# The planner of a fused RWKV7 + GELU kernel gets other constants, other load order and other places for its padding

## The chip, the cores and the metric

The kernel runs on one core of a Trainium2 chip. All times are device microseconds of that core, from the runs and from one profiled execution. The kernel before took 725.19 us (median of three runs, 724.26 to 728.75).

The engines are named as the profile names them: PE is TensorE (PEld its weight loads), DVE is VectorE, ACT is ScalarE, POOL is GpSimd, SP is SyncE, which here does nothing but issue DMAs. "Issue" in the profile is time in which an engine waited for nothing that the profile shows.

## The reference

An RWKV7 recurrence over 768 time steps for 4 x 8 heads of size 40, then an MLP of 320 -> 2048 -> 320 with quick GELU over its 3072 tokens. All in float32; the MLP's weights arrive as float64.

```python
for t in range(S):
    kt, vt, rt = (k[:, :, t], v[:, :, t], r[:, :, t])
    wt, at, bt = (w[:, :, t], a[:, :, t], b[:, :, t])
    y[:, :, t] = np.einsum('bhd,bhde->bhe', rt, state)
    Sa = np.einsum('bhde,bhe->bhd', state, at)
    state_decay = state * wt[:, :, None, :] - np.einsum('bhd,bhe->bhde', Sa, bt)
    state = state_decay + np.einsum('bhd,bhe->bhde', vt, kt)
...
h = x @ w_in
g = h * (1.0 / (1.0 + np.exp(-1.702 * h)))
return (g @ w_out).astype(np.float32)
```

## The kernel before

**Tiling.** The recurrence is cut into 12 chunks of 64 steps; each chunk has two units (a unit is half of the batch), so there are 24 units. Unit i needs the state that unit i-2 left. For each unit the kernel forms cumulative decays (`ps_cum`, `ps_cumc`), scores (`ps_A`, `ps_N`, `ps_RV`), the inverse of a triangular matrix in five levels (`ps_level`, then `ps_Q`, `ps_T`), the read of the old state (`ps_zT`, `ps_rz`), the right-hand side (`ps_B`), its solution (`ps_X`) and the output (`ps_y`). The output goes to DRAM (`x_dram`, line 917) and comes back transposed (`xT_all`, line 921). When both units of a chunk are back, the MLP of the chunk can run: 160 x 2 matmuls `ps_up`, the GELU on ACT (`g`), and twice 64 x 2 matmuls `ps_down`.

**Weights.** The MLP's weights come in eight pieces of 1.31 MB each, as float64 (lines 398 to 448). Each piece is loaded into a spare place, turned by ACT (line 422), and then by DVE in five steps (lines 426, 430, 431, 434 and 438). Line 438 is the last one: the piece is usable after it. Pieces 0 to 3 are for `ps_up`, pieces 4 to 7 for `ps_down`. All of this happens in the first 130 us.

**Loads.** A unit's inputs are `ak`, `time`, `b`, `rv` and `RV`, issued by SP in the function `load`; `logw` and `wc` are issued in `load_w`. `ak`, `b` and `rv` fill only 40 of each 64 rows; the other rows stay zero, so the two buffers of each are zeroed once at the start (`padded`, line 306). Before, the three first buffers are zeroed on DVE and the three second ones on POOL, as the last thing of POOL's constants. SP issues in order: a DMA that has to wait for a buffer holds all that follow it.

**The order of the work.** The kernel is fully unrolled, and the order of the instructions on every engine is worked out when it is built. The class `Plan` holds a list of tasks with durations and dependences and plays them through on a picture of the chip: `order` starts, at each moment, the task of best rank that is ready. `paced` repeats this four times with other release times for the MLP's tasks and keeps the pass whose picture ends first. Then the instructions are issued in the order of that pass. So the constants of the picture do not run on the chip; they only decide what comes after what. On the chip each engine runs its list in order, and stops where an operand is not there yet.

The picture has four parts that matter here. `FETCH` is the time in which TensorE's instruction stream gets its next block of `BLOCK` = 256 instructions, and `BESIDE` lengthens it by a share of the time that data transfers run beside it. `LATENCY`, `RATE` and `SPREAD` give the time from the issue of a DMA to its landing. `BEGIN` says from when each engine is free. A task has a `release` before which it may not start; for loads it is zero before.

```python
BLOCK, FETCH, BESIDE, AHEAD = 256, 3550.0, 0.4, 300.0
...
BEGIN = {"PE": 0.0, "ACT": 3300.0, "DVE": 4100.0, "POOL": 9500.0, "SP": 800.0}
LATENCY, RATE, SPREAD = 1200.0, 400.0, 1.3
```

Of the kernel before, what the change touches and what calls it, by code (L numbers as in the profile page):

```python
# [23 lines left out]
ACT = mybir.ActivationFunctionType  # L24
# [34 lines left out]
class Plan:  # L59
# [2 lines left out]

    BLOCK, FETCH, BESIDE, AHEAD = 256, 3550.0, 0.4, 300.0
    DELAY = {"PE": 300.0, "DVE": 60.0, "ACT": 60.0, "POOL": 150.0, "SP": 800.0}

    BEGIN = {"PE": 0.0, "ACT": 3300.0, "DVE": 4100.0, "POOL": 9500.0, "SP": 800.0}
    LATENCY, RATE, SPREAD = 1200.0, 400.0, 1.3

    def __init__(self, slots, pairs):
        self.slots, self.pairs = slots, pairs
        self.tasks, self.made, self.used, self.of_pair = [], {}, {}, {}

    def add(self, rank, engines, fn, reads=(), uses=(), writes=(), room=(), pair=None, most=None, size=0):

        t = Task(rank, engines, fn, pair, most, size)
        for key in uses:  # L80
            self.used.setdefault(key, []).append(t)
        for key in reads:
            t.after.update(self.made[key])
            self.used.setdefault(key, []).append(t)
        for name, n in (*writes, *room):
            if name in self.slots:
                old = (name, n - self.slots[name])
                t.after.update(self.made.get(old, ()), self.used.get(old, ()))
        for key in writes:
            self.made.setdefault(key, []).append(t)  # L90
        if pair is not None:
            writers = self.of_pair.setdefault(pair, [])
            t.after.update(o for o in writers if "PE" in o.engines)
            writers.append(t)
        t.after.discard(t)
        self.tasks.append(t)

    def order(self):
# [11 lines left out]
        running, last = [], {}  # L110

        def fits(t):
            if t.pair is None or t.pair in held:
# [7 lines left out]
        issued, begun, shared = 0, 0.0, 0.0  # L121

        def fetch(at):
            took = self.FETCH
            for _ in range(3):
                beside = sum(max(0.0, min(y, at + took) - max(x, at)) for x, y in running[-8:])
                took = self.FETCH + self.BESIDE / self.SPREAD * beside
            return took

        def unread(t, e):  # L130

            return max((x + 60.0 for o, x in last.get(t.pair, {}).items() if o != e), default=0.0) if t.pair is not None and e != "PE" else 0.0

        def fetched(t, start):

            at, left, ns, block = start, t.instr, t.engines["PE"] / t.instr, begun
            room = self.BLOCK - issued % self.BLOCK
            while left >= room:
                at += room * ns
                left -= room  # L140
                at = block = max(at, block + fetch(block))
                room = self.BLOCK
            return at + left * ns, block

        def ahead(t):

            return (issued % self.BLOCK + t.instr) * fetch(begun) / self.BLOCK - (now + t.engines["PE"] - begun)

        while coming or able:
            while coming and coming[0][0] <= now:  # L150
# [2 lines left out]
            took = None  # L153
# [12 lines left out]
            t = took  # L166
# [2 lines left out]
            end = now + t.engines[e]  # L169
            if e == "PE":  # L170
                end, begun = fetched(t, now)
                issued += t.instr
            if e == "POOL" or e == "DVE" and t.sbuf:

# [2 lines left out]
            free[e] = end  # L177
            if e == "SP":
                wire = max(wire, end + self.LATENCY)
                running.append((wire, wire + self.SPREAD * t.size / self.RATE))  # L180
                end = wire = running[-1][1]
            if t.pair is not None:
                if e != "PE":
# [42 lines left out]
def rwkv7_gelu_quick(ctx: ExitStack, tc: tile.TileContext, time_d, v_d, w_d, wc_d, ak_d, b_d, rv_d, w_in, w_out, out):  # L226
    nc = tc.nc
# [31 lines left out]
    def single(name, shape):  # L259
        return const.tile(shape, FP32, tag=name, name=name)  # L260
# [44 lines left out]
    def padded(engine, t):  # L305
        engine.memset(t, 0.0)
# [10 lines left out]
    nc.vector.tensor_add(two32, one32, one32)  # L317
    padded(nc.vector, b_t[0])
    padded(nc.vector, rv_t[0])

    def select(t, compare, base, sign, fill):

# [13 lines left out]
    for t in logw_t:  # L336
        nc.gpsimd.memset(t[:, DM:], 0.0)

    starts = single("starts", [128, 8, 33])
    nc.gpsimd.memset(starts, 1.0)  # L340
    nc.gpsimd.memset(starts[:, :, 0], 0.0)

    quads, within = single("quads", [128, 2, 32]), single("within", [128, 2, 32])
    nc.gpsimd.memset(quads, 0.0)
# [9 lines left out]
        for p in HALF:  # L354
            select(t[p, :64], ALU.is_gt, 0, 1, 0.0)

    for t in ak_t[1], b_t[1], rv_t[1]:
        padded(nc.gpsimd, t)

    def mask(t):  # L360
        return t.unsqueeze(1).unsqueeze(1).to_broadcast([128, 2, 4, 64])
# [100 lines left out]
    def load_w(i):  # L462
        for name, of, src, n in (("wc", wc_of, wc_d, 528), ("logw", logw_of, w_d, DM))[i < BY_PE:]:
            plan.add(-2 if i == 2 else 10 * i - 30, {"SP": 350.0}, lambda t, of=of, src=src: nc.sync.dma_start(of(i), src[i]),
                     writes=[(name, i)], size=128 * n * 4)

    def load(i):
        for name, of, src, n in (("ak", ak_of, ak_d, 1024), ("time", time_of, time_d, 2 * DM), ("b", b_of, b_d, 512),
                                 ("rv", rv_of, rv_d, 1024), ("RV", RV_of, v_d, 320)):
            rows = [slice(p.start, p.start + D) for p in HALF] if name in ("ak", "b", "rv") else [slice(0, 128)]  # L470

            def go(t, name=name, of=of, src=src, rows=rows):
                for p in rows:
                    dst = of(i)[p, 8:].rearrange("p g j n -> p (g j n)") if name == "RV" else of(i)[p]
                    nc.sync.dma_start(dst, src[i, p])
# [612 lines left out]
```

## Time and profile before

| | us |
|---|---|
| median of 3 runs | 725.19 |
| the profiled execution, device time | 728.5 |
| its span, first to last instruction | 726.7 |
| PE busy in the span | 677.6 |
| DVE busy | 430.0 |
| ACT busy | 356.8 |
| POOL busy | 187.9 |
| mean granted TensorE clock | 0.978 |

The profile page gives for the whole span the busy time of each engine, then slices, DMA queues, the chain of work that ended last, and groups of instructions by line. A table of stretches gives the same busy times for chosen parts of the span; the numbers in brackets are counts of instructions, PEclk is the granted TensorE clock as a share of full speed, then come the mean busy share of the 16 DMA engines and the GB/s that they moved. The chain of waits lists start, duration and what ran, one piece after another.

A busy PE is not PE at its peak, since matmuls overlap and their ends are modelled. Where a number of "PE work" is given, it is the number of matmuls times the time from start to start that the same form has in long runs at full clock: `ps_up` x160 take 8.63 us (54 ns each), `ps_down` x224 15.07 us (67 ns), `ps_y` x64 1.43 us (22 ns), and the forms of 64 columns and less x32 0.46 us (14.5 ns).

### The profile page before, as it was taken

The numbers are of one execution on the slowest core, as the hardware profiler recorded it, in microseconds if no ns is written. First come the engines' busy times: TensorE is split into PE (matmuls) and PEld (weight loads), VectorE is DVE, ScalarE is ACT, GpSimd is POOL, SyncE is SP. The second block draws the span as 40 slices with busy tenths as digits, with TensorE's granted clock in tenths as the row PEclk, the third lists the DMA queues.
The fourth block names the chain that finished last, engine by engine and source line by source line (L and its number), as shares of the span: only waits on it lengthen the run. The fifth ranks groups of instructions, "written<-read, shape, count | busy, mean of one in ns | idle before, by whom it ended". The sixth has DMA issues, their size and how long they took to land.

```text
span 726.7 us, 43527 instructions
## 1 busy us (share of the span) xinstructions
PE 677.6 (93%) x20256; PEld 572.5 (79%) x20256; DVE 430.0 (59%) x739; ACT 356.8 (49%) x705; POOL 187.9 (26%) x260
## 2 busy tenths in 40 slices
PE   4566997999999999999999999999999989999997
PEld 4555885799788789888888878887889978897564
DVE  6578888956667666666756655755666556431000
ACT  4455655557554554545465455457446446342120
POOL 8104143432431331330350320431530310200000
PEclk9879998999999999999999999999999999999999
DMA  7963542332251341351450440441340230110000
GB/s 216 351 251 93 165 124 86 107 96 78 91 145 55 109 120 49 88 158 32 119 136 22 116 130 31 119 118 39 120 112 23 85 95 5 40 49 30 18 5 20
DMA packets 31861, 69.82 MB, mean 96 GB/s; under 512 B 5056, under 2 KB 14272, under 8 KB 30656
## 3 DMA queue, kind: packets, MB, share of 16 engines
q1 hardware_dynamic: 31680, 67.03, 30.5%
q8 instruction: 159, 2.61, 1.4%
q14 instruction: 22, 0.18, 0.1%
HBM read 59.15 MB, written 7.86 MB: 92 GB/s over the span
## 4 chain that ended last, share of the span: by engine, by line
PE 83%; DVE 5%; issue 3%; ACT 3%; DMA 3%; POOL 2%; SPq 1%; POOLq 0%; DVEq 0%; ACTq 0%
PE ps_down L275 28%; PE ps_up L275 26%; PE ps_level L275 8%; PE ps_y L275 5%; PE ps_B L275 4%; PE ps_X L275 2%; DMA ak<-in_ak 2%; PE ps_Q L275 2%; PE ps_N L275 1%; PE ps_T L275 1%; PE ps_rz L275 1%; PE ps_A L275 1%; PE ps_RV L275 1%; PE ps_zT L275 1%; PE ps_cum L275 1%
## 5 line engine op out<-in xcount | busy, mean ns | idle before, releaser
L275 PE MATMUL ps_up<-xT_all,w_sb 64*64 64x256 f32 x3840 | 249.1, 378 | 2.6 <-ACT g L942 1.5
L275 PE MATMUL ps_down<-w_sb,g 64*64 64x320 f32 x3072 | 244.4, 434 | 3.1 <-DVE w_sb L438 2.5
L275 PEld LDWEIGHTS ps_up<-xT_all,w_sb 64*64 64x64 f32 x3840 | 160.6, 133 | 26.7 <-ACT g L942 1.8
L275 PEld LDWEIGHTS ps_down<-w_sb,g 64*64 64x64 f32 x3072 | 136.2, 134 | 45.3 <-issue 3.1
L670 ACT ACTIVATE EX<-ES,quads 128x256 f32<-128x256 f32 x116 | 52.6, 501 | 49.7 <-DVE ES L665 49.3
L591 POOL TENSOR_TENSOR kh<-time,G 128x320 f32<-128x320 f32 x24 | 22.0, 918 | 185.3 <-PE ps_y L275 91.4
L942 ACT ACTIVATE g<-ps_up 128x1024 f32<-128x1024 f32 x48 | 49.1, 1023 | 40.4 <-PE ps_up L275 40.1
L275 PEld LDWEIGHTS ps_level<-W,EX 64*64 64x64 f32 x2560 | 57.3, 134 | 7.4 <-ACT EX L670 1.4
L716 DVE TENSOR_TENSOR E<-two,ps_level 128x256 f32<-128x256 f32 x80 | 33.2, 415 | 40.3 <-ACT W L714 39.8
L275 PE MATMUL ps_level<-W,EX 64*64 64x64 f32 (+1 forms) x2560 | 55.7, 218 | 0.7 <-ACT EX L670 0.3
L714 ACT COPY W<-ps_level 128x512 f32<-128x512 f32 x51 | 29.8, 585 | 44.0 <-PE ps_level L275 43.9
L275 PE MATMUL ps_level<-PT,EX 64*64 64x64 f32 (+2 forms) x1280 | 36.6, 251 | 11.4 <-DVE EX L686 7.2
L968 DVE TENSOR_TENSOR ob<-ob,ps_down 128x320 f32<-128x320 f32 x24 | 11.6, 484 | 59.4 <-ACT ob L966 59.1
L275 PEld LDWEIGHTS ps_level<-PT,EX 64*64 64x64 f32 x1280 | 34.3, 152 | 15.2 <-DVE EX L686 7.0
L907 POOL TENSOR_TENSOR x<-zr,FT 128x128 f32<-128x128 f32 x84 | 42.8, 539 | 10.4 <-ACT zr L899 10.2
L583 POOL TENSOR_TENSOR ak<-ak,FT 128x512 f32<-128x512 f32 x21 | 27.3, 1299 | 53.2 <-DMA ak<-in_ak 26.2
L845 ACT COPY B<-ps_B 128x416 f32<-128x416 f32 x36 | 18.2, 506 | 44.1 <-PE ps_B L275 43.6
L275 PE MATMUL ps_y<-RV,kh 64*64 64x104 f32 x768 | 36.4, 252 | 2.3 <-DVE M L861 2.2
L665 DVE STREAM_TRANSPOSE ES<-E 128x256 f32<-128x256 f32 x80 | 35.6, 445 | 3.9
L275 PE MATMUL ps_y<-M,bh 64*64 64x104 f32 x768 | 36.5, 252 | 1.3 <-issue 1.3
L275 PEld LDWEIGHTS ps_y<-RV,kh 64*64 64x64 f32 x768 | 30.1, 134 | 6.4 <-DVE M L861 2.4
L861 DVE TENSOR_TENSOR M<-ps_X,later 128x832 f32<-128x832 f32 x24 | 24.5, 1021 | 17.6 <-PE ps_X L275 17.6
(140 smaller groups left out, 1132.9 us busy)
## 6 DMA issues: line engine op xcount, KB each, us to landing
ak<-in_ak SPq DMA_DIRECT2D x48, 160.0 KB
time<-in_time SPq DMA_DIRECT2D x24, 320.0 KB
rv<-in_rv SPq DMA_DIRECT2D x48, 160.0 KB
xT_all<-x_dram SPq DMA_DIRECT2D x48, 160.0 KB
wc<-in_wc SPq DMA_DIRECT2D x20, 264.0 KB
logw<-in_w SPq DMA_DIRECT2D x24, 160.0 KB
b<-in_b SPq DMA_DIRECT2D x48, 80.0 KB
RV<-in_v SPq DMA_DIRECT2D x24, 160.0 KB
```

What stands on the lines that cost most here:

```text
L275: nc.tensor.matmul(o, lhsT, rhs, start=start, stop=True, skip_group_check=True)
L583: plan.add(R, {"DVE": 690.0, "POOL": 1270.0, "sbuf": True}, lambda t: of(t.engine).tensor_mul(ahT(), ahT(), FT_of(i)), reads=T("ak", "FT") ...
L591: plan.add(R + 4, {"POOL": 870.0, "DVE": 490.0, "sbuf": True}, lambda t, n=n, dst=dst: of(t.engine).tensor_mul(dst(i)[:, :, :D], by_head(t ...
L665: plan.add(rank, dve(256), lambda t: nc.vector.transpose(ES(n), source(t)), writes=[key("ES", n, 6)], **reads)
L670: nc.scalar.activation(dst[:, :, h], ES(n), ACT.Copy, scale=quads[:, h, :1])
L714: plan.add(rank, any2(512), lambda t: copy(t.engine)(tiles_of(W(n + 1)), blocks(psum(t, ""), 64)), writes=[key("W", n + 1, 5)], pair=pair)
L716: plan.add(rank, dve(256), lambda t: nc.vector.tensor_sub(tiles_of(E(n + 1)), every(two32, [128, 2, 4, 32]), blocks(psum(t, ""), 64)[:, :, ...
L845: plan.add(R, any2(416), lambda t: copy(t.engine)(dst(), psum(t, "")[:, :, :208]), writes=[("Bv", i)] if x and c > 0 else T("B"), pair=(na ...
L861: plan.add(R + 1, dve(832), lambda t: nc.vector.tensor_tensor(M_of(i).rearrange("p (j b) n -> p b j n", b=2), psum(t, "")[:, :, :416].rear ...
L907: of(t.engine).tensor_mul(x[:, b ^ u, b], both(i)[:, at, :64], FT_of(i)[:, at])
L942: plan.add(-45, act(1024), lambda t: nc.scalar.activation(g_of(c * NQ + q).rearrange("p m r n -> p r m n"), psum(t, "").rearrange("p r (m ...
L968: plan.add(-45, dve(320), lambda t: nc.vector.tensor_add(ob_of(serial), ob_of(serial), psum(t, "")[:, 1, :DM]), reads=[("ob", serial)], wr ...
```

## The change

It alters the planner's picture, the order and release of loads, and the engines and places of six zeroings. It adds no matmul and takes none away: both kernels have 20,256 matmuls and as many weight loads.

- `FETCH` goes from 3550 to 3528. The share of transfers beside a fetch goes from 0.4/1.3 = 0.31 to 0.35, and to 0.63 for transfers over 1 MB (the weights).
- A matmul task takes twice its time in the picture when TensorE was busy for less than 0.45 of the 2.6 us before it (`takes`).
- `LATENCY` goes from 1200 to 2010, `RATE` from 400 to 417 bytes per ns; DVE is free from 5500 instead of 4100, POOL from 10000 instead of 9500.
- In `load`, `time` goes from the second place to the last.
- The first loads of `ak`, `b` and `rv` get a release time: when the zeroing of their buffer is over (`CLEAR`).
- Of the second buffers, `b` and `rv` are now zeroed on DVE, and `ak` on POOL ahead of most constants; `starts` is filled last.

```diff
-    BLOCK, FETCH, BESIDE, AHEAD = 256, 3550.0, 0.4, 300.0
+    BLOCK, FETCH, AHEAD = 256, 3528.0, 300.0
+    BESIDE, LARGE, BESIDE_LARGE = 0.35, 1e6, 0.63
+    COLD, WINDOW, SHARE = 2.0, 2600.0, 0.45
...
-    BEGIN = {"PE": 0.0, "ACT": 3300.0, "DVE": 4100.0, "POOL": 9500.0, "SP": 800.0}
-    LATENCY, RATE, SPREAD = 1200.0, 400.0, 1.3
+    BEGIN = {"PE": 0.0, "ACT": 3300.0, "DVE": 5500.0, "POOL": 10000.0, "SP": 800.0}
+    LATENCY, RATE, SPREAD = 2010.0, 417.0, 1.3
...
-                beside = sum(max(0.0, min(y, at + took) - max(x, at)) for x, y in running[-8:])
-                took = self.FETCH + self.BESIDE / self.SPREAD * beside
+                took = self.FETCH + sum(w * max(0.0, min(y, at + took) - max(x, at)) for x, y, w in running[-10:])
...
+        def takes(t, start):
+
+            busy = sum(max(0.0, y - max(x, start - self.WINDOW)) for x, y in worked[-60:])
+            return t.engines["PE"] * (self.COLD if busy < self.SHARE * self.WINDOW else 1.0)
+
         def fetched(t, start):
 
-            at, left, ns, block = start, t.instr, t.engines["PE"] / t.instr, begun
+            ns = takes(t, start) / t.instr
+            at, left, block = start, t.instr, begun
...
-            return (issued % self.BLOCK + t.instr) * fetch(begun) / self.BLOCK - (now + t.engines["PE"] - begun)
+            return (issued % self.BLOCK + t.instr) * fetch(begun) / self.BLOCK - (now + takes(t, now) - begun)
...
+                worked.append((now, min(end, now + takes(t, now))))
...
-                running.append((wire, wire + self.SPREAD * t.size / self.RATE))
+                running.append((wire, wire + self.SPREAD * t.size / self.RATE, self.BESIDE_LARGE if t.size > self.LARGE else self.BESIDE))
...
     padded(nc.vector, b_t[0])
     padded(nc.vector, rv_t[0])
+    padded(nc.vector, b_t[1])
+    padded(nc.vector, rv_t[1])
...
-    starts = single("starts", [128, 8, 33])
-    nc.gpsimd.memset(starts, 1.0)
-    nc.gpsimd.memset(starts[:, :, 0], 0.0)
+    padded(nc.gpsimd, ak_t[1])
...
-    for t in ak_t[1], b_t[1], rv_t[1]:
-        padded(nc.gpsimd, t)
+    starts = single("starts", [128, 8, 33])
+    nc.gpsimd.memset(starts, 1.0)
+    nc.gpsimd.memset(starts[:, :, 0], 0.0)
...
+    CLEAR = {("ak", 0): 2000.0, ("b", 0): 3100.0, ("rv", 0): 4100.0, ("ak", 1): 4500.0, ("b", 1): 4600.0, ("rv", 1): 5500.0}
+
     def load(i):
-        for name, of, src, n in (("ak", ak_of, ak_d, 1024), ("time", time_of, time_d, 2 * DM), ("b", b_of, b_d, 512),
-                                 ("rv", rv_of, rv_d, 1024), ("RV", RV_of, v_d, 320)):
+        for name, of, src, n in (("ak", ak_of, ak_d, 1024), ("b", b_of, b_d, 512), ("rv", rv_of, rv_d, 1024),
+                                 ("RV", RV_of, v_d, 320), ("time", time_of, time_d, 2 * DM)):
...
-                     size=sum(p.stop - p.start for p in rows) * n * 4)
+                     size=sum(p.stop - p.start for p in rows) * n * 4, release=CLEAR.get((name, i), 0.0))
```

More of the change, by code (lines that the diff above doesn't have):

```diff
@@ L73, in __init__, with add @@
         self.tasks, self.made, self.used, self.of_pair = [], {}, {}, {}
-    def add(self, rank, engines, fn, reads=(), uses=(), writes=(), room=(), pair=None, most=None, size=0):
+    def add(self, rank, engines, fn, reads=(), uses=(), writes=(), room=(), pair=None, most=None, size=0, release=0.0):
         t = Task(rank, engines, fn, pair, most, size)
+        t.release = release
         for key in uses:
@@ L109, in order @@
         able, now, wire, out, many = [], 0.0, 0.0, [], set()
-        running, last = [], {}
+        running, last, worked = [], {}, []
         def fits(t):
```

## The prediction

> **What bounds the kernel now.** I read the engine totals and the DMA queues of the page first, then the table of stretches, then the chain of waits.
>
> ```profile
> PE 677.6 (93%) x20256; PEld 572.5 (79%) x20256; DVE 430.0 (59%) x739; ACT 356.8 (49%) x705; POOL 187.9 (26%) x260
> ...
> q8 instruction: 159, 2.61, 1.4%
> ```
>
> PE is the bound. It streams 2 x 20,256 instructions in 159 blocks (255 each, 16.4 KB).
>
> ```profile
> 0.00:18.00 18.00, 8.60 (x276) 7.40 (x280) 11.70 (x20) 7.63 (x26) 14.76 (x51) 1.00 0.73 214
> 18.00:36.00 18.00, 10.72 (x339) 9.76 (x331) 10.27 (x14) 7.55 (x16) 1.78 (x3) 0.81 1.01 352
> 36.00:54.00 18.00, 11.79 (x382) 10.38 (x383) 13.56 (x18) 10.67 (x23) 0.28 (x1) 0.72 0.71 261
> 54.00:72.00 18.00, 11.98 (x473) 10.93 (x472) 15.84 (x21) 10.72 (x23) 7.18 (x10) 0.91 0.30 86
> 72.00:90.00 18.00, 16.11 (x453) 13.71 (x457) 15.00 (x22) 10.71 (x23) 3.25 (x4) 0.91 0.51 167
> 90.00:109.00 19.00, 18.82 (x520) 17.18 (x516) 16.18 (x18) 9.71 (x13) 8.61 (x8) 1.00 0.45 126
> 109.00:127.00 18.00, 12.84 (x416) 9.60 (x411) 14.69 (x20) 10.26 (x22) 5.89 (x5) 0.81 0.24 87
> 127.00:145.00 18.00, 17.21 (x544) 13.42 (x539) 16.33 (x30) 9.54 (x20) 6.97 (x10) 1.00 0.36 105
> 145.00:345.00 200.00, 199.25 (x6269) 175.74 (x6264) 128.33 (x239) 108.42 (x206) 59.43 (x70) 1.00 0.32 93
> ```
>
> The third column is PE. It is busy for 108.1 of the first 145 us (37 idle) and for 199.25 of the next 200. From 145 to the end only some 12 us are idle. In start-to-start terms the kernel has 647 us of PE work; span, less 3.8 us before the first matmul and some 5 at the end, leaves 71 us lost: 57 before 145 us, 14 after it. The change cannot touch the 647. It can win or lose in the 57 and the 14.
>
> The chain shows what the 57 are:
>
> ```profile
> 8.18 0.94 POOL ak L306
> 9.14 0.30 SPq L475
> ...
> 11.97 5.58 DMA rv<-in_rv
> 17.59 0.63 PE ps_RV L275 x27
> ...
> 19.54 3.36 issue
> ...
> 27.12 2.82 issue
> ...
> 113.33 2.33 DVE extra L434
> ...
> 117.50 1.75 DVE w_sb L438
> 119.30 4.54 PE ps_down L275 x32
> ...
> 128.81 1.50 DVE w_sb L438
> ```
>
> Unit 1's loads wait for POOL's zeroing of `ak`; then PE stops for 3.36 and 2.82 us with nothing to wait for, each in the middle of one group of matmuls, while the DMA engines are full: late instruction blocks. At 113 to 130 us `ps_down` waits for DVE to finish weight pieces 6 (119.2) and 7 (130.3), and runs at half clock after it.
>
> **What the Trainium skill says.** "Runtime: NRT & Kernel Launch", section Instruction fetch mechanics: instructions come in blocks of 256, by the sequencer's own DMA queue, mostly hidden. The block size agrees (255); "hidden" does not: 3.36 and 2.82 us. "TensorE: Matmul & The Clock Gate", section What's actually happening: half clock after an idle window of some 3.4 us. The trace has 0.72 of the clock in the stretch 36 to 54. "DMA: Bandwidth & Descriptors", section Anatomy of one DMA: a fixed 2.0 us and the bytes. The first `logw` was issued at 0.81 to 1.22 and ACT read it at 3.21, which agrees. "GPSIMD Engine Reference", section 4.1 Engine selection: about 2x VectorE for two inputs; here 1.27 us against 0.69 for the same product on `ak`.
>
> **The change, part by part.** What it really moves is the order of instructions, which is fixed at build time and can be compared directly.
>
> *Zeroing and first loads.* POOL zeroes `ak` of unit 1 about 4.6 us earlier (it ends near 4.5, not 9.1); DVE takes 0.48 + 0.91 us more, so its two clearings of `zr` end at 7.3 instead of 5.9, just after the 7.03 at which it first used `ak`. SP now issues `RV` and `time` of unit 0 ahead of `ak`, and another `RV` ahead of `rv`: about 490 KB more on the wire before unit 0's `ak`, and some 330 KB more before its `rv` (one `RV` and `logw`). At the 214 GB/s of this stretch that is 0.8 to 2.3 us later; I take 0.9. The product of `k` and decay goes to POOL (1.27 instead of 0.69 us, +0.6), but TensorE does `ps_RV` and `ps_N` before it needs it. Unit 0: +0.9 us, between 0 and +2. Unit 1's `rv` no longer waits for POOL: it lands some 2 to 3 us earlier, and PE's 1.1 us of waits on that DMA (0.70 and 0.38) go. What is late next is the block that PE got at 22.9; that is set by transfers of the same bytes, so I count nothing won by the wire's start. Sum here: 0, between -2 and +2. Weight pieces move up in SP's list, ahead of unit 2's inputs (pieces 1 to 4 are issued back to back): pieces 2 to 4 land 2 to 5 us sooner, unit 2's `ak` and `b` later (near 41 instead of 32 to 34 us), just before `ps_N` of unit 2 ran at 45.4. Their issues hold nothing but the loads behind them.
>
> *Up to the first `ps_up`.* Both orders have the same 29.5 us of PE work up to unit 2's `ps_B` (77.2 us on the clock). Then the orders part: before, `ps_up` starts after 30.7 us of work (78.4 us on the clock); after, 36.5 us, with unit 3's state read and `ps_B` pulled ahead of it. These 768 instructions are three blocks; at 3.5 us a block (estimate: the fastest distance between block transfers in the trace, 3.5 us) 10.7 us for 6.9 us of work. On the other side unit 2's state product now stands in DVE's list before weight piece 3, not after: it was at 69.4, and can be near 63, so `ps_B` of unit 2 can be some 3 us earlier. I take: the first `ps_up` near 84 us, with as much work done as the kernel before had at 84. Zero, between -3 and +4.
>
> *The wait for weights.* Here I expect the win. With full-clock PE work as the ruler, `ps_down` on piece 6 stands at 64.3 before and 68.4 after; on piece 7 at 70.7 and 72.6. So PE has 4.1 and 1.9 us more to do before it needs them. DVE's list holds 90.9 and 98.6 us of work up to the ends of pieces 6 and 7 before, 93.4 and 103.7 after (row durations from the trace: 0.82, 1.65, 1.5 and 1.46 us for the steps of a piece). DVE starts earlier, though: at the second `M` it has done 50.8 us of its list instead of 43.9, at about the same time (63 to 64 us), since pieces 1 and 2 are in SBUF sooner. With the same idle time as before from there on, piece 7 is ready at 64.4 + 52.9 + 12.5 = 129.8, against 130.3. Lag of the clock behind work: 130.3 - 70.7 = 59.6 us before, 129.8 - 72.6 = 57.2 after. Win 2.4 us; if DVE idles less because PE feeds it steadily, 5; if it idles as much as now in total, 0. I take 3.
>
> *The steady part.* Of the 14 us lost after 145 us about 4.7 are near places where the chain runs through a load of `ak`:
>
> ```profile
> 591.45 4.10 DMA ak<-in_ak
> ```
>
> The same took 3.79 at 372.6 and 4.83 at 425.4. In the picture before, such a load (two issues, 327 KB) lands 1200 + 1063 ns after its issue, with the change 2010 + 1021. So its product on DVE or POOL, which holds that engine's list while it waits, is put 0.77 us later: at three places up to 2.3 us, and I take 1. `time` as a unit's last load: in the steady part loads are issued as buffers come free, so I count 0; it is read only by `kh` and `bh`, over 90 us of work later. `BESIDE`, `FETCH` and `takes` only shuffle here: the same matmuls in another interleaving, with PE 99.6% busy from 145 to 345. Between -3 and +4.
>
> **Sum.** 0 + 0 - 3 - 1 = -4 us against the profiled span of 726.7, so 722.7, and 724.5 for that execution's device time (728.5, 1.8 around the span). That execution was 3.3 above the median of the runs; on the median, 725.2 - 4 = **721**.
>
> **Rivals.** *More is won (712, chance 0.19).* If unit 3's early work takes the wait for pieces 6 and 7 away entirely (the 109 to 127 stretch lost 9 us in start-to-start terms, the next one 2), and the steady part wins its 2.3: -13. For it: units 3 and 4 are 5 to 13 us of work earlier in the new order, so PE has other work there. Against it: DVE is over 80% busy from 54 to 145 us and has the same pieces to do.
>
> *Slower (733, chance 0.19).* One mechanism: DVE's list. Output `x` of unit 0 now stands behind piece 2 (46.7 us of DVE work ahead of it instead of 37.8), and the long stretch of small matmuls before the first `ps_up` has no MLP work to fill its waits; each gap of PE brings the half clock back. If that stretch runs as 54 to 72 did (9.1 us of work in 18), its 6.9 us take 13.7 instead of 10.7, DVE's later inputs slip with it, and piece 7 is ready at 137: 7 to 8 us slower. It decides if the first `ps_up` starts later than about 88 us.
>
> *The picture is better and nothing comes of it (725, chance 0.14).* The orders differ, but piece 7 is ready at 130 to 132 and the steady part is a new draw of the same small losses.
>
> **How the numbers follow.** Forecast 0.48 (717 to 725), the rivals as above. A measurement of this kernel can tell about 1% from no change, that is 7.3 us: faster is below 718, slower above 732.4. Faster: 0.19 and a tenth from the forecast's lower edge, 0.28. Slower: 0.19 of the rival, some of it below the bound, plus bad draws of the steady part: 0.20. Same: 0.52. The range 711 to 734 takes in both rivals up to 2 in 10 left out.
>
> **What would show it.** Unit 0's first product on `ak` at 7.3 to 8 us; no wait of `ps_RV` on `in_rv` near 17; late blocks still near 20 and 28 us; the first `ps_up` at 82 to 86; the line-438 step of piece 7 ending at 126 to 131 and fewer than 6 us of idle PE in 109 to 127; PE idle after 145 us at 9 to 13 us. The prediction is wrong if DVE stops at a weight step before 30 us because its piece has not landed, if unit 2 waits for `ak` near 45 us, or if the steady part's idle time moves by over 4 us.

## The result, and the profile after

The changed kernel takes 729.10 us (median of 20 runs, 725.24 to 735.66) where the kernel before takes 725.34 us beside it (20 runs, 720.68 to 728.85). The ratio is 1.0052, with a 95% interval of 1.0029 to 1.0075. A second measurement gave 729.33 against 724.48 us, a ratio of 1.006 (1.0039 to 1.0081). So the change costs about 4 us, half a per cent. I had forecast a gain of 4. All ratios here are formed from fast runs alone (within 1.5 per cent of the fastest run of the same kernel) and are therefore not the quotient of the medians beside them, which matters most for the run with `LATENCY` 1990, where six of 14 runs fall out and the medians alone would give 1.015.

The page of the changed kernel has the same TensorE (PE) work and the same instruction blocks as before:

```profile
PE 679.9 (93%) x20256; PEld 580.0 (80%) x20256; DVE 444.1 (61%) x759; ACT 346.5 (47%) x661; POOL 208.3 (29%) x275
...
q8 instruction: 159, 2.61, 1.5%
```

The table of stretches of the changed kernel, with the columns as in the prediction (bounds and length; busy time of PE, weight load, DVE, ACT, POOL; granted clock, DMA share, GB/s):

```profile
0.00:18.00 18.00, 7.43 (x224) 6.63 (x224) 11.94 (x18) 5.96 (x17) 10.53 (x45) 1.00 0.74 238
18.00:36.00 18.00, 11.01 (x379) 9.12 (x380) 14.52 (x20) 12.06 (x28) 3.98 (x4) 0.85 1.00 386
36.00:54.00 18.00, 14.05 (x440) 13.06 (x436) 16.04 (x18) 10.54 (x23) 6.32 (x5) 0.59 0.66 206
54.00:72.00 18.00, 11.96 (x479) 11.23 (x483) 17.73 (x24) 6.78 (x19) 5.89 (x6) 0.91 0.29 83
72.00:90.00 18.00, 11.50 (x381) 9.96 (x374) 11.37 (x18) 10.50 (x23) 7.98 (x9) 0.72 0.68 193
90.00:109.00 19.00, 18.95 (x588) 15.53 (x584) 17.25 (x23) 9.07 (x17) 5.90 (x7) 1.00 0.39 105
109.00:127.00 18.00, 17.83 (x504) 12.98 (x500) 16.90 (x21) 15.56 (x22) 9.27 (x8) 1.00 0.32 107
127.00:145.00 18.00, 15.98 (x452) 11.43 (x448) 16.20 (x26) 10.31 (x24) 6.01 (x6) 1.00 0.39 113
145.00:345.00 200.00, 195.93 (x6184) 168.41 (x6180) 132.96 (x241) 103.94 (x193) 57.90 (x70) 1.00 0.31 90
```

PE's busy time shows a swap: 72 to 90 falls from 16.11 to 11.50 us, and 109 to 127 rises from 12.84 to 17.83. It is `ps_up` that moved: before, 149 of its matmuls start between 72 and 90 us and none between 109 and 127; after, it is none and 116. From 145 to 345 us PE is busy for 195.93 us instead of 199.25.

Busy time is stretched by a slow clock (the 32 `ps_down` at 119.30 us in the chain of before take 4.54 us at a granted clock of 0.50, against 2.15 at the pace of the long runs), so I use the prediction's ruler for all that follows. The matmuls are sorted by their start. From the distance between two starts I take the time that a matmul of that width has at full clock by the kernel's own `pe`: (columns/1.2 + 3)/4 ns, at least 14.5 ns. What is left over is called **excess** here. The full-clock work is 647.2 us in every whole kernel. Excess in us, by stretch:

| stretch | before | after | after, second profile |
|---|---|---|---|
| 0–18 | 9.3 | 10.8 | 11.0 |
| 18–36 | 12.6 | 10.2 | 10.2 |
| 36–54 | 9.8 | 12.2 | 11.3 |
| 54–72 | 9.6 | 6.5 | 8.4 |
| 72–90 | 3.8 | 11.4 | 11.2 |
| 90–109 | 0.4 | 0.6 | 0.2 |
| 109–127 | 9.0 | 0.6 | 0.6 |
| 127–145 | 2.0 | 2.9 | 2.9 |
| 145–end | 14.1 | 18.3 | 16.8 |
| sum | 70.6 | 73.5 | 72.6 |

The chain of waits of the changed kernel, early part (start, duration, what):

```profile
3.23 0.92 DVE rv L315
4.16 0.06 SPq L487
...
9.92 6.38 DMA rv<-in_rv
...
16.35 0.82 PE ps_RV L284 x27
...
80.17 0.95 PE ps_level L284 x18
81.13 3.66 issue
84.79 1.08 PE ps_level L284 x17
...
91.43 1.29 PE ps_up L284 x24
...
119.66 0.86 PE ps_up L284 x16
120.52 1.08 PE ps_down L284 x16
```

Four things are to be seen. Unit 1's `rv` no longer waits for POOL, but for DVE's zeroing and a load of 6.38 us, and PE still waits for it. PE stands still for 3.66 us in the middle of one group of `ps_level` with nothing to wait for: a late instruction block, here at the time when weight piece 6 (1.31 MB, issued at 73.48 us) and seven smaller transfers behind it fill the DMA engines (from 78 to 82 us the trace has their share at 1.04). The trace has the block itself: a packet of 16,384 bytes on the instruction queue q8 ends at 83.34, and PE goes on at 84.79. At the stops in the chain of before at 19.5 and 27.1 us, and at those of the changed kernel at 27, 570 and 612 us, PE also goes on 1.3 to 1.5 us after such a packet has ended. The first `ps_up` comes at 91.25 us instead of 78.42. And at 120 us `ps_up` is followed by `ps_down` without a stop, where the kernel before waited for a weight piece until 119.3 us.

### The profile page after: what moved, and what is told of

Same layout as the page of the kernel before. It is cut to its first block, busy times and chain, and to the rows that moved or that the text cites. A ratio compares the mean times of both kernels' runs of the same rounds, so it can differ in the third digit from the quotient of the medians.

```text
span 729.5 us, 43551 instructions
## 1 busy us (share of the span) xinstructions
PE 679.9 (93%) x20256; PEld 580.0 (80%) x20256; DVE 444.1 (61%) x759; ACT 346.5 (47%) x661; POOL 208.3 (29%) x275
## 4 chain that ended last, share of the span: by engine, by line
PE 83%; DVE 7%; ACT 5%; issue 3%; DMA 2%; POOL 0%; SPq 0%; ACTq 0%; DVEq 0%
PE ps_down L284 27%; PE ps_up L284 26%; PE ps_level L284 9%; PE ps_y L284 5%; PE ps_B L284 4%; PE ps_X L284 3%; PE ps_T L284 2%; PE ps_Q L284 1%; PE ps_zT L284 1%; PE ps_rz L284 1%; PE ps_RV L284 1%; PE ps_A L284 1%; PE ps_N L284 1%; DVE EX L698 1%; DMA rv<-in_rv 1%
## 5 line engine op out<-in xcount | busy, mean ns | idle before, releaser
L284 PE MATMUL ps_up<-xT_all,w_sb 64*64 64x256 f32 x3840 | 254.5, 378 | 1.5 <-DVE E L728 0.8
L284 PEld LDWEIGHTS ps_up<-xT_all,w_sb 64*64 64x64 f32 x3840 | 162.7, 133 | 24.1 <-issue 3.0
L284 PEld LDWEIGHTS ps_down<-w_sb,g 64*64 64x64 f32 x3072 | 143.3, 133 | 40.7 <-issue 3.8
L954 ACT ACTIVATE g<-ps_up 128x1024 f32<-128x1024 f32 x48 | 49.2, 1025 | 44.8 <-PE ps_up L284 44.3
L682 ACT ACTIVATE EX<-ES,quads 128x256 f32<-128x256 f32 x108 | 49.2, 504 | 43.8 <-DVE ES L677 43.3
L603 POOL TENSOR_TENSOR kh<-time,G 128x320 f32<-128x320 f32 x22 | 20.3, 921 | 131.6 <-PE ps_y L284 58.5
L726 ACT COPY W<-ps_level 128x512 f32<-128x512 f32 x51 | 29.9, 586 | 58.7 <-PE ps_level L284 55.0
L980 DVE TENSOR_TENSOR ob<-ob,ps_down 128x320 f32<-128x320 f32 x24 | 11.6, 484 | 63.0 <-ACT ob L978 62.7
L284 PE MATMUL ps_level<-PT,EX 64*64 64x64 f32 (+2 forms) x1280 | 36.6, 250 | 14.1 <-DVE EX L698 7.4
L284 PEld LDWEIGHTS ps_level<-PT,EX 64*64 64x64 f32 x1280 | 33.8, 150 | 19.5 <-issue 10.4
L857 ACT COPY B<-ps_B 128x416 f32<-128x416 f32 x39 | 19.7, 506 | 57.2 <-PE ps_B L284 56.9
L919 POOL TENSOR_TENSOR x<-zr,FT 128x128 f32<-128x128 f32 x80 | 45.1, 592 | 0.4 <-DVE zr L909 0.4
L684 POOL TENSOR_TENSOR T<-ES,quads 128x512 f32<-128x512 f32 x14 | 17.9, 1276 | 71.3 <-DVE ES L677 71.3
L600 POOL TENSOR_TENSOR ak<-ak,GT 128x512 f32<-128x512 f32 x22 | 36.8, 1674 | 0.1
```

Of the source, the lines that this page charges most:

```text
L284: nc.tensor.matmul(o, lhsT, rhs, start=start, stop=True, skip_group_check=True)
L600: plan.add(R, {"DVE": 690.0, "POOL": 1270.0, "sbuf": True}, lambda t: of(t.engine).tensor_mul(khT(), khT(), GT_of(i)), reads=T("ak", "GT") ...
L603: plan.add(R + 4, {"POOL": 870.0, "DVE": 490.0, "sbuf": True}, lambda t, n=n, dst=dst: of(t.engine).tensor_mul(dst(i)[:, :, :D], by_head(t ...
L682: nc.scalar.activation(dst[:, :, h], ES(n), ACT.Copy, scale=quads[:, h, :1])
L684: of(t.engine).tensor_mul(dst, ES(n).unsqueeze(2).to_broadcast([128, 8, 2, 32]), quads.unsqueeze(1).to_broadcast([128, 8, 2, 32]))
L726: plan.add(rank, any2(512), lambda t: copy(t.engine)(tiles_of(W(n + 1)), blocks(psum(t, ""), 64)), writes=[key("W", n + 1, 5)], pair=pair)
```

## The experiments

Two kinds of edit are used. One changes constants of the planner, which gives another order. The other keeps the planner's order and moves single tasks in it, by this helper ahead of the loop that emits the tasks (a task is named by what it writes):

```
+    spot = lambda name: next(k for k, t in enumerate(tasks) if name in t.names)
+    def behind(name, other):
+        t = tasks.pop(spot(name))
+        tasks.insert(spot(other) + 1, t)
     for t in tasks:
         t.fn(t)
```

All ratios below are to the kernel before, measured on the same chip in the same series. Where I compare two edited kernels of different series, I compare their ratios.

### The stop at 81 us

```
+    behind(("wt", 6), ("rv", 5))
+    behind(("rebased", 6), ("g", 1))
```

> The changed kernel's order with one load moved: weight piece 6 (1.31 MB) is issued behind unit 5's rv instead of ahead of unit 4's ak, and ScalarE's first step on it behind the second GELU. Theory (a block of instructions comes late because the piece fills the DMA engines at 74 to 79 us): the 3.66 us stop of TensorE at 81 us goes, unit 1's returned x lands some 4 us sooner (about 77.5), the stretch 72 to 90 has about 4 us less excess and the whole is 2 to 4 us shorter than the changed kernel, about 726. Rival (the stretch is bound by its own chain of small dependent products): the stop at 81 us is filled by other waits, the first ps_up stays at 90 to 91.5 us, and the time stays within 1 us of 729.

Measured: 727.21 us, ratio 1.004 (1.0019 to 1.006). In the chain of waits of this kernel the stop at 81 us is gone, and it runs through other waits (L555 alone is a table load of ScalarE):

```profile
80.34 1.28 ACT L555
...
84.86 0.47 DMA rv<-in_rv
...
85.39 1.52 issue
...
89.09 1.29 PE ps_up L285 x24
...
92.33 0.63 issue
```

The first `ps_up` starts at 88.9 instead of 91.25 us, and the excess of 72 to 90 falls from 11.4 to 9.1 us. The same pair of matmuls that stood apart by 3.66 us in the chain (4.0 us of excess) is now 1.78 us late. But one profile of each kernel doesn't show that the load made the stop. Six profiles have piece 6 in its old place and the changed order up to 109 us: two of the changed kernel, one of its cut, one without late loads and two with ScalarE's tasks moved, all below. In them this pair has 4.00, 3.18, 2.63, 1.69, 3.18 and 1.55 us of excess, while the share of the DMA engines in the 4 us before the stop is 0.95 to 1.04. With the piece moved that share is 0.68, and the stop is no shorter than in two of the six. Nor does the excess of 72 to 90 us set it apart, 8.8 to 11.4 us in the six. And by 128 us any lead is gone: `ps_level` behind `ps_cum` starts at 128.9 us in both kernels (128.19 + 0.72 and 128.10 + 0.72). PE stopped at 91.2 us for 1.75 (the moved load is then on its way) and at 113.3 for 1.19. Against the changed kernel's 1.0052 and 1.006, the gain is about 1 us and not certain. So the theory's cause is not shown, and its price was too high.

### Which part of the change does it

The first kernel keeps the new order of loads and the new zeroing, with the new `BEGIN` that goes with it, and takes the old picture otherwise:

```
-    BLOCK, FETCH, AHEAD = 256, 3528.0, 300.0
-    BESIDE, LARGE, BESIDE_LARGE = 0.35, 1e6, 0.63
-    COLD, WINDOW, SHARE = 2.0, 2600.0, 0.45
+    BLOCK, FETCH, AHEAD = 256, 3550.0, 300.0
+    BESIDE, LARGE, BESIDE_LARGE = 0.4 / 1.3, 1e6, 0.4 / 1.3
+    COLD, WINDOW, SHARE = 1.0, 2600.0, 0.45
...
-    LATENCY, RATE, SPREAD = 2010.0, 417.0, 1.3
+    LATENCY, RATE, SPREAD = 1200.0, 400.0, 1.3
```

> The change without its new picture of the machine: the order of loads in a unit, the zeroing and its release times stay; the costs of fetch, load and clock are those of before. Theory (the new picture puts the first ps_up late, and takes the waits for ak away): the first ps_up is again at 76 to 82 us, loads of ak stand in the chain of waits again, unit 1's rv lands near 16.3; time 723 to 727. Rival (the load order is what made it late): the first ps_up is at 88 to 92 us, time 728 to 731.

The second is the kernel before with the new picture alone (its `BEGIN` stays the old one):

```
-    BLOCK, FETCH, BESIDE, AHEAD = 256, 3550.0, 0.4, 300.0
+    BLOCK, FETCH, AHEAD = 256, 3528.0, 300.0
+    BESIDE, LARGE, BESIDE_LARGE = 0.35, 1e6, 0.63
+    COLD, WINDOW, SHARE = 2.0, 2600.0, 0.45
...
-    LATENCY, RATE, SPREAD = 1200.0, 400.0, 1.3
+    LATENCY, RATE, SPREAD = 2010.0, 417.0, 1.3
```

> The new picture of fetches, loads and cold clock alone, with the load order and zeroing of before. Theory (the new picture puts the first ps_up late and takes the waits for ak away): the first ps_up at 86 to 92 us, no load of ak in the chain of waits after 145 us, less than 3 us of excess in 109 to 127; time 726 to 731. Rival (the load order is what made it late): first ps_up at 76 to 82 us, time 721 to 725.

And the third is the kernel before with the load part of the picture alone:

```
-    LATENCY, RATE, SPREAD = 1200.0, 400.0, 1.3
+    LATENCY, RATE, SPREAD = 2010.0, 417.0, 1.3
```

> The kernel before with the load part of the new picture alone: LATENCY 2010 and RATE 417 instead of 1200 and 400. Theory (with loads that land later in the picture no engine's list waits for ak, and that is worth the 2 us and more that the prediction gave it): no load of ak in the chain of waits after 145 us, excess there below 12 us, time 721 to 724. Rival (a new order has its own stops, whatever loads cost in the picture): 725 to 731 with 14 us or more after 145 us, with or without loads of ak in the chain.

Measured: 731.94 us, ratio 1.0116 (1.0071 to 1.0161); 730.83 us, 1.0087 (1.0054 to 1.0119); 731.07 us, 1.0086 (1.0052 to 1.012). Each part alone measured slower than the whole change, though the intervals touch. The first `ps_up` is at 73.4, 78.0 and 73.8 us, so the theories on it fell (the second kernel's rival had the place right and the time wrong), and its time doesn't order the kernels: the changed kernel has the latest first `ps_up` and is the fastest of these four. No load of `ak` is in the chain of waits after 145 us in any of them, with the old LATENCY (the first kernel) as with the new. So it doesn't take later landings in the picture, as the prediction's steady part and my first theory had it, to be rid of these waits; another order will do. For the third kernel, with 16.2 us of excess after 145 us, the rival holds.

### Where on the time axis the loss lies

```
+    done = [sum(t.instr for t in tasks[:k + 1]) // 2 for k in range(len(tasks))]
+    tasks = tasks[:next(k for k, n in enumerate(done) if n >= 3340) + 1]
     for t in tasks:
         t.fn(t)
```

For the changed kernel the number is 3400 instead of 3340.

> The kernel before, cut off: its list of tasks ends after TensorE's first 3340 matmuls or just over, which the profiled execution had issued at 144.6 us; everything later, and with it most of the output, is left out. It and the changed kernel's cut are compared by the time that each needs beyond the full-clock duration of its own matmuls, over many executions. Theory (to 145 us the changed order is ahead, and the 4 us are lost after that): this beyond-time is 1 to 3 us longer than the changed kernel's. Rival (one profiled execution misleads, and the changed order is behind already here): it is 2 to 4 us shorter.

> The changed kernel, cut off after TensorE's first 3400 matmuls or just over (145.0 us in the profiled execution); everything later, and with it most of the output, is left out. Theory: beyond the full-clock duration of its matmuls it needs 1 to 3 us less than the cut of the kernel before. Rival: 2 to 4 us more.

Measured: 147.29 us for the cut of before with 84.55 us of matmul work, 146.07 us for the cut of the changed kernel with 86.10. That is 62.7 and 60.0 us beyond the work. By the letter of the expectation the changed order is 2.8 us ahead. But in the two profiles the end of the kernel comes 4.1 us after the end of the last matmul in the one (143.0 to 147.1) and 1.0 in the other (148.8 to 149.8); what is still under way at the cut differs. Taken off the medians, these tails leave 58.7 and 59.0 us beyond the work. But the second profile is of an execution of 151.52 us, over 5 above its median, so its tail need not hold for the others, and the cuts decide nothing. Profiles of whole kernels that share an order up to 145 us say more: 56.5, 52.6, 53.4 and 50.9 us of excess for the order of before, 55.2, 55.8 and 54.1 for the changed one. Within one order single executions differ by up to 5.6 us; the means are 53.4 and 55.0. So up to 145 us nothing was won that these runs can show, and a loss of 1 or 2 us there can't be excluded.

After 145 us the orders do part, and in one stretch. From 145 to 345 us the order of before has 3.1, 5.2, 1.7 and 4.8 us of excess in these profiles (the moves in two of them come later), the changed one 7.9, 7.3 and 7.2. From 345 us to the end the two profiles of whole, unmoved orders with all loads have 11.0 before and 10.4 after (9.5 in the second), and without late loads 6.2 and 5.9, which is no loss. So the 4 us are lost, in the main, between 145 and 345 us.

### Extra table loads on ScalarE

In the changed kernel ScalarE loads a table 42 times, before 38. The additional ones come where a GELU (`g`) stands between `exp_channel` and `G` of one unit, in units 5, 7 and 18. The chain of waits of the changed kernel at unit 7 (L954 and L568 alone are table loads):

```profile
161.89 1.28 ACT L954
...
163.18 1.03 ACT g L954
...
164.22 1.28 ACT L568
...
165.52 0.45 ACT G L568
...
166.01 0.69 PE ps_N L284 x32
```

```
+    for i in (5, 7, 18):
+        behind(("G", i), ("FT", i))
+        behind(("log", i + 2), ("G", i))
```

> The changed kernel's order with ScalarE's exponent G and the next logarithm put directly behind exp_channel for units 5, 7 and 18, where a GELU stands between them. Theory (extra table loads cost TensorE time): table loads fall from 42 to about 38, the stops of TensorE near 163 to 166 us (1.9 us) and 463 to 469 us (2.0 us) go, the time falls by 2 to 4 us, to about 726. Rival (ScalarE has room, and the stops are only the places where something else is late): table loads fall, but the excess after 145 us stays at 17 to 19 us and the time within 1 us of 729.

Measured: 728.18 us, ratio 1.0071 (1.0048 to 1.0095), so nothing gained; the rival holds. Tables are loaded 34 times. The stops near 463 us shrink from 2.0 to under 0.3 us, but at unit 7 PE stops just as long as before, once for 2.16 us instead of twice for 0.95. The GELU now comes behind `G` and the logarithm, and PE waits for it:

```profile
164.70 1.28 ACT L955
...
166.00 1.03 ACT g L955
...
167.08 0.69 PE ps_RV L285 x32
```

So I put the GELU first, in a later run:

```
+    for i, q in ((5, 2), (7, 5), (18, 27)):
+        behind(("FT", i), ("g", q))
```

> The changed kernel's order with exp_channel of units 5, 7 and 18 moved behind the GELU that stood between it and G on ScalarE, so that exp_channel, G and the logarithm stand together behind it. Theory (the stops that recur at 163 to 166 and 463 to 469 us are lost time, 3.6 us in the first profile, 2.9 in the second): both go, 2 to 4 us faster than the changed kernel, a ratio of 1.000 to 1.003 to before. Rival (later exponents of those units stop TensorE elsewhere): 1.004 to 1.007.

Measured: 727.81 us, ratio 1.0046 (1.0025 to 1.0066). The rival holds. Near 466 us one stop of 1.29 us stands in place of 2.0 in all, and at unit 7 PE stops once again, for 2.04 us, now because `G` comes late (L555 is a table load):

```profile
166.12 1.02 ACT g L955
...
167.16 1.28 ACT L555
...
169.82 0.33 ACT G L569
...
170.19 0.69 PE ps_N L285 x32
```

ScalarE needs some 4 us there for two things that PE waits for, a GELU and `G`. Whichever comes second is late, and taking table loads away in front of one of them moves the stop to the other.

### The stops behind a load of `ak`, in the kernel before

If those stops are lost time, taking them out of the kernel before by hand must make it faster:

```
+    behind(("ahT", 15), ("EX", 63))
+    behind(("khT", 17), ("sums", 19))
+    behind(("ahT", 23), ("EX", 105))
+    behind(("G", 19), ("FT", 19))
+    behind(("log", 21), ("G", 19))
```

> The kernel before with five of its tasks moved by a few places in its own order and nothing else: the products of ak with a decay for units 15, 17 and 23 stand behind the next tasks of their engine that do not need that load (POOL's EX, DVE's A and scans, DVE's RV and EX), and G and the logarithm of unit 19 and 21 stand directly behind exp_channel. In the profile of before TensorE stops for 1.18, 1.29, 2.24 and 1.32 us at these four places (377, 432, 595 and 488 us). Theory (the stops behind a load of ak are lost time, as the prediction's steady part has it): 3 to 6 us faster than before, 718 to 722. Rival (the lost time is handed on to the next wait): within 1.5 us of before, and the excess after 145 us stays at 13 to 15 us.

Measured: 726.05 us, ratio 1.0009 (0.9985 to 1.0032). The excess after 145 us is 12.7 us against 14.1. The stops at 432 and 595 us are gone (1.29 and 2.24 us before), the one at 488 grew from 1.32 to 2.53 because the GELU came later, and a new one of 0.89 came up at 595, between other matmuls. So `exp_channel` of unit 19 was put behind that GELU, in place of the last two moves:

```
-    behind(("G", 19), ("FT", 19))
-    behind(("log", 21), ("G", 19))
+    behind(("FT", 19), ("g", 28))
```

> The kernel before with the three products on ak moved as in the run with four places, and exp_channel of unit 19 moved behind the GELU ahead of which it stood. Theory (recurring stops are lost time): the stop at 488 us goes as well as the three behind ak, and it is 2 to 5 us faster than before, ratio 0.993 to 0.997. Rival (handed on): ratio 0.998 to 1.002.

Measured: 724.04 us, ratio 1.0011 (0.999 to 1.0031), with 13.5 us of excess after 145 us, a stop of 1.83 us at that place and late blocks of 1.08 and 1.15 us at 189 and 264 us. The rival holds both times. My prediction gave such places up to 2.3 us.

### Transfers or the order of the engines

From unit 8 on the loads of `ak`, `b` and `rv` are left out in both orders; the products work on what the buffers hold.

```
             def go(t, name=name, of=of, src=src, rows=rows):
+                if i >= 8 and name in ("ak", "b", "rv"):
+                    return
                 for p in rows:
```

> The kernel before in its own order, but from unit 8 on the loads of ak, b and rv are left out and the products work on what is in the buffers: the numbers are no longer the reference's from there on, the instructions of the engines are the same except for SP's DMAs. Theory (transfers make the stops after 145 us): this kernel gains 3 to 6 us against before, and the changed order (next run) 6 to 10, so that the two end within 1.5 us of each other. Rival (the order of the engines makes them): both gain the same, 0 to 4 us, and the changed order stays 3 to 5 us slower.

> The changed kernel in its own order, with the loads of ak, b and rv left out from unit 8 on as in the run before this. Theory (transfers): within 1.5 us of that run. Rival (order of the engines): 3 to 5 us slower than it.

Measured: 720.12 us, ratio 0.9929 (0.9904 to 0.9954), and 724.96 us, ratio 1.0016 (0.9997 to 1.0035), both beside 724.48 us of before. Each order gains 4.4 us, a little more than the rival had, and the changed one stays 4.8 us behind. So the rival holds: these loads don't make the difference, and what is left is the order in which the engines work. The tables of stretches, first of the order of before, then of the changed one:

```profile
145.00:345.00 200.00, 199.52 (x6367) 173.68 (x6363) 130.06 (x243) 109.26 (x207) 56.71 (x69) 1.00 0.22 63
345.00:545.00 200.00, 197.38 (x6150) 159.54 (x6146) 124.82 (x230) 109.94 (x215) 63.98 (x81) 1.00 0.24 65
```

```profile
145.00:345.00 200.00, 195.99 (x6191) 167.73 (x6185) 131.67 (x241) 103.44 (x193) 58.78 (x71) 1.00 0.22 63
345.00:545.00 200.00, 198.28 (x6126) 168.03 (x6121) 126.14 (x230) 102.26 (x192) 69.89 (x87) 1.00 0.24 65
```

PE is idle for 0.5 us in the first 200 us of the one and for 4.0 in the other, as it was with all loads (0.75 and 4.07). In the next 200 us the changed order is idle for less, 1.7 against 2.6. After 145 us the excess is 7.9 and 13.1 us.

### Which stops belong to the order

> The changed kernel unedited, once more beside the kernel before. Every theory expects a ratio of 1.003 to 1.007. If the stops belong to the order, its second profile has them at the same instructions: near 27, 81, 163 to 166 and 463 to 469 us; if they belong to single executions, fewer than half of them come back.

Measured: ratio 1.006 (1.0039 to 1.0081). The chain at unit 7 in this second profile is the same, 0.55 us later:

```profile
162.44 1.28 ACT L954
...
163.73 1.02 ACT g L954
...
164.77 1.28 ACT L568
...
166.07 0.45 ACT G L568
```

The late blocks near 25 and 82.7 us come back too (3.63 and 3.18 us of excess), at the same matmuls as in the first profile. After 145 us the stops between two different groups return, save one of 0.92 us at 624. In us of excess, first profile, second, and the kernel without late loads: 163.3 and 165.0 us: 0.95 + 0.94, 0.94 + 0.94, 0.94 + 0.94; 212: 0.91, 0.92, 0.95; 325: 0.96, 0.96, 0.96; 360: 0.73, 0.73, 0.76; 463 to 469: 2.0, 2.0, 2.0. Those up to 325 us make 3.8 us, about what the stretch from 145 to 345 us lost. The stops in the middle of one group, which are late blocks, do not: at 570.4 us 1.23 in the first profile and at 611.9 1.04, at either place under 0.1 in the other two. So the hand-offs between engines belong to the order, and the late blocks of the steady part to the execution.

### Orders near before and near after

Is this the content of the change, or does any other order cost as much? Two constants of the kernel before were moved by an amount that says nothing of the machine:

```
-    BLOCK, FETCH, BESIDE, AHEAD = 256, 3550.0, 0.4, 300.0
+    BLOCK, FETCH, BESIDE, AHEAD = 256, 3528.0, 0.4, 300.0
```

> The kernel before with one constant of the picture set as the change sets it: FETCH 3528 instead of 3550 ns, 0.6 per cent, which says nearly the same of the machine, but gives another order from TensorE's 167th task of 1080 on. Theory (the content of the change makes the time): no content, so within 1.5 us of the kernel before. Rival (the order of before is a good draw of many, and any new order costs some us): 2 to 7 us slower, and not through the first 40 us, which stay as they were.

```
-    LATENCY, RATE, SPREAD = 1200.0, 400.0, 1.3
+    LATENCY, RATE, SPREAD = 1220.0, 400.0, 1.3
```

> The kernel before with LATENCY 1220 instead of 1200 ns, 20 of the 810 that the change adds; another order from TensorE's 17th task on. Theory (the content of the change makes the time): within 1.5 us of the kernel before. Rival (a new order is a new draw): 2 to 7 us slower.

Measured: 728.63 us, ratio 1.0045 (1.0019 to 1.0072); 725.72 us, ratio 1.0039 (1.0016 to 1.0062). Both are slower, as the rival had it. The same was done around the changed kernel, one constant in each run:

```
-    BLOCK, FETCH, AHEAD = 256, 3528.0, 300.0
+    BLOCK, FETCH, AHEAD = 256, 3550.0, 300.0
```

> The changed kernel with FETCH back at 3550 instead of 3528 ns; another order from TensorE's 36th task on. Theory (the order of before is one good draw, and the changed picture is no better or worse than the old one): somewhere in 723 to 733, like the two draws near before (725.7 and 728.6), and as far from the changed kernel as those are from before. Rival (the changed picture makes better or worse orders in itself): within 1.5 us of the changed kernel, 727.5 to 730.5.

```
-    LATENCY, RATE, SPREAD = 2010.0, 417.0, 1.3
+    LATENCY, RATE, SPREAD = 1990.0, 417.0, 1.3
```

> The changed kernel with LATENCY 1990 instead of 2010 ns; another order from TensorE's 56th task on. The same two theories: somewhere in 723 to 733 (a draw), or 727.5 to 730.5 (the picture decides).

Measured: 739.85 us, ratio 1.0206 (1.0163 to 1.0249); 736.17 us, ratio 1.0099 (1.0067 to 1.013). Both lie outside 723 to 733, further out than either theory had it. That 22 ns move the time by 1.5 per cent, three times what the whole change did, and 20 ns by about as much as the change, is what the theory of draws says. In these two profiles the excess after 145 us is 26.5 and 25.0 us, while up to 145 us it is 56.6 and 53.9; from 145 to 345 alone it is 17.0 and 13.4.

So nine planner orders were measured, the one of before among them. The other eight are slower, by 0.4 to 2.1 per cent, and the change with 0.5 is the third best of those eight. In the profiles of all eight the excess from 145 to 345 us is 6.5 us or more, against 1.7 to 5.2 in four of the order of before. Two things this doesn't settle. The five orders planned with a `LATENCY` of 1990 or 2010 cost 0.5 to 2.1 per cent, the three others 0.4 to 1.2; that is too few to say whether the new picture gives worse orders on average. And why the order of before is the best is not known; if it was once chosen from several by its time, any new order would be expected to lose.

## Why the prediction was wrong

**Zeroing and first loads: 0.** The sum held, its parts did not. Unit 0's first product on `ak` came at 8.43 us where I gave 7.3 to 8, and unit 1's `rv` landed at 16.31 instead of 17.55, less early than I had it, so the wait of `ps_RV` on `in_rv` that I wanted gone is still in the chain. To 18 us the excess is 1.5 us more than before, from 18 to 36 it is 2.4 less, and to 36 us it is 21.0 against 21.9.

**Up to the first `ps_up`: zero, between −3 and +4.** This step failed. The first `ps_up` came at 91.25, not near 84, and the excess up to 90 us was 51.1 against 45.1, that is 6 us worse. I had put the three extra blocks at the fastest distance seen. In place of that the DMA engines were busier from 72 to 90 us (share 0.68, before 0.51), one block came 3.66 us late in a stretch without MLP work, and the clock fell to 0.72. The loss to 90 us is in every profile: 40.4 to 45.1 us of excess in five of the order of before, 50.5 to 52.2 in six of the changed one.

**The wait for weights: −3.** The mechanism was right and the size wrong. From 109 to 127 us 8.4 us were won, because PE had other work when the pieces came (piece 7 was ready at 128.4; I gave 129.8). These two are one exchange: the small products pulled ahead of 90 us pushed `ps_up` back, and it is `ps_up` that filled 109 to 127. Their sum, with the rest up to 145 us, shows no gain (53.4 us of excess on average before, 55.0 after). I had priced the two halves as if they were independent.

**The steady part: −1.** This is the step that failed where the sign is concerned. I took three waits for `ak` out and put nothing in their place. The waits did go. But with the old LATENCY too they are gone in two of three other orders, and in the third (`FETCH` 3528) one of 3.48 us is left; and without them the kernel before is no faster. In their place came hand-offs that stop PE at the same instructions in each execution. The profiles have 2.7 and 4.2 us more excess after 145 us, where I had 1 less; with late loads out of both orders it is 5.2, and the times are 4.8 us apart. My range for this step ended at +4, so what was measured lies at its edge, and the value had the wrong sign.

**The rivals.** The slower one is not what happened, though the time of the first `ps_up` had passed its point of 88 us: piece 7 was ready at 128.4, not at 137. "The picture is better and nothing comes of it" named the mechanism, a new draw of the same small losses, but I took a draw to cost nothing on average. Eight draws cost 0.4 to 2.1 per cent. The kernel before was not an average order but the best of those measured; the prediction had no means to see that from one profile.

**What stays open.** Which decision of the planner makes the changed order's hand-offs worse is not settled. The places are known, but of the repairs none of those on ScalarE gave more than about 1 us, and those at 212, 325 and 360 us, where PE waits between `ps_A` and `ps_RV`, for DVE's `W` and `E`, and for ScalarE's copy of `zT`, were not tried. Nor was the loss of 6 us and more up to 90 us taken apart: that piece 6 makes it was not shown. No version here that does the whole work beats the kernel before.

## What to carry to other kernels

Where a planner writes the order of a whole kernel, a change of its constants must be priced as a new order, not as the sum of the stalls that it is meant to mend; constants moved by 20 or 22 ns show in two or three runs how far orders scatter, and where the current one stands among them. A stop in the chain of waits is worth its length only if what comes next is not late as well: none of the stops taken away here shortened the kernel by its own length. Two profiles of the same kernel tell the stops of the order from those of the execution, and before a stop is called mended, the unmended kernel's own profiles must show how much it varies.

## What was not expected of the hardware

A late instruction block in the early part comes back at the same matmul in every execution of an order, but its size does not: at the pair of `ps_level` near 81 us PE stood for 1.55 to 4.00 us of excess in six profiles with a DMA share of 0.95 to 1.04 just before, and for 1.78 with weight piece 6 moved away and a share of 0.68. In the steady part, with DMA shares near 0.3, late blocks of up to 1.2 us come and go from one execution to the next. At the stops looked at, PE went on 1.3 to 1.5 us after the end of the block's packet. And leaving out the loads of `ak`, `b` and `rv` from unit 8 on, which lowers the DMA share from 145 to 345 us from 0.31 to 0.22, gains 4.4 us in either order, though in the changed one no load of `ak` is in the chain of waits; by what way is open.
